# Turning K with 64x64 matmuls against the unit matrix in place of eight 128x128 transposes

## The chip, the cores and the metric

The kernel runs on one core of one Trainium2 chip. The metric is the device time of one execution in microseconds (us); lower is better. Five engines work side by side: TensorE (PE in the profile; PEld is its weight load), VectorE (DVE), ScalarE (ACT), GpSimd (POOL) and SyncE (SP, which issues most of the DMAs). Each works through its own list of instructions in order, and semaphores hold an instruction back until what it needs is there.

## The reference

An RWKV-6 attention is followed by a feed-forward block. All data are fp32.

```python
B, H, S, D = 4, 8, 768, 48
for t in range(S):                                   # per (b, h); state is D x D
    y[t]  = r[t] @ (state + outer(u * k[t], v[t]))
    state = w[t][:, None] * state + outer(k[t], v[t])
x = y.transpose(0, 2, 1, 3).reshape(B * S, H * D)    # 3072 x 384
h = x @ w_in                                         # 384 -> 2048
g = h * erf(softplus(h))
out = g @ w_out                                      # 2048 -> 384
```

## The kernel before

The sequence is cut into chunks of 128 tokens and the batch into pairs, which makes 12 steps, `s` = 0 to 11. A step handles one chunk of `NJ` = 2 batch elements with 8 heads each. Two heads share the 128 partitions: the heads of half `e` = 0 stand on partitions 0 to 47 and those of half `e` = 1 on 64 to 111. So `r`, `k` and `w` lie as [128, `JP` = 8, 128 tokens] with the head dimension on the partitions, `v` as [128 tokens, 16, 48], and `rows(e)` names the 48 partitions of a half.

**The attention of a step.** Inside a chunk, tokens are split into two halves `h` of 64 (`HC`). Products between tokens are formed by levels, from neighbouring tokens (level 1) to the halves of a 64 (level 6, `LOG`). For each level TensorE forms 32 small products, each in a 64x64 part of its array (`level_products`, L436); VectorE scales the operands for the next level (`scale`, L252) and VectorE or ScalarE takes the wanted part into `own` (`take_level`, L448 and L455). Then

- `from_own` (L470) multiplies `own` with `v` into the output `y`, 16 matmuls for each of its two calls (`swap` = 1 and 0);
- K is turned, so that tokens stand on the partitions: L663 into PSUM, and one ScalarE copy (L667) into `kT`;
- `state_part` (L522) multiplies `kT` with `v`, 32 matmuls, and VectorE and POOL make the state at the middle and at the end of the chunk from it (L690 to L695);
- `through_state` (L496) adds what the state gives to `y`, and the sum is copied into `xT` (L503 to L506, with small DMAs at L510).

Steps 0 to 4 (`DIRECT` = 4) do this in `attend`, and they alone turn K on TensorE. Steps 5 to 11 run `attend_late`, in which VectorE and POOL form the near terms from rows and `kT` comes by DMA (L405). At the head of `attend_late` for steps 6 to 11 stand, directly behind each other, `from_own` of the step before (L470), `level_products` (L436), the second `from_own` (L470) and `through_state` (L496) of the step before.

**The feed-forward block** runs in between, in pieces that `place` hands out: `hidden` (L731) forms the 16 tiles of `h` with three matmuls each for 256 tokens; ScalarE copies them out (L740) and applies softplus and erf (L713, L716); VectorE multiplies (L720); `project` (L754) multiplies with `w_out`, eight matmuls at a time. `hidden` works for step s - 1 and `project` for step s - 3. In steps 0 to 3 the two weight matrices are converted from 64-bit words as well (`convert`: ScalarE L207 and L209, VectorE L216 and L219, POOL L223). In step 0 a few extra matmuls on constant data stand at L623 and L631.

**What sets the order.** The whole program runs under `tc.manual_schedule`: each engine's instructions stand in the order in which the Python code emits them, with no planner. Around the changed lines, TensorE's order in step 2 is `from_own` (swap 1), the turn, twelve matmul rows of L731, `state_part`, `from_own` (swap 0), twelve rows of L731, `through_state`. In steps 3 and 4 there are 24 and 36 rows of L731 behind the turn; in step 0 there is one matmul of L631 instead. PSUM results of the attention go to two buffers of two banks each, taken in turn by `products`.

An fp32 matmul shows in the trace as two weight loads and two matmul rows; a transpose as one of each.

Of the kernel before, what the change touches and what calls it, by code (L numbers as in the profile page):

```python
# [17 lines left out]
P = 128  # L18
EP = 64
HC = 64  # L20
NC = 2
# [39 lines left out]
def kernel(  # L61
# [14 lines left out]
    nc = tc.nc  # L76
    PSUM = bass.MemoryType.PSUM

    n_steps, _, _, JP, C = rkw.shape
    NH, D = v.shape[2:]  # L80
    NP = JP // NJ
    NE = NH // JP
# [32 lines left out]
    ident = const.tile([P, P], FP32, name="ident")  # L115
# [12 lines left out]
    def products(shape):  # L128


        n = 0 if turns["converting"] else turns["next"]
        turns["next"] = 1 - n
        return ps_p.tile(shape, FP32, name=f"pp{n}")
# [31 lines left out]
    def near_log(s):  # L165
        return NEAR_LOG - (s == DIRECT)
# [70 lines left out]
    def rows(e, n=D):  # L237
        return slice(e * EP, e * EP + n)
# [7 lines left out]
    def scale(s, level):  # L246

        in_t, tots = loaded[s][0], ready[s][1]
        half, nb = 1 << (level - 1), JP * C >> level
        n = 1 if s > DIRECT and level == LOG else 2  # L250
        halves = view(in_t[:, 0:2], half, [[JP * C - half, n], [2 * half, nb], [1, half]])
        nc.vector.tensor_mul(  # L252
            halves, halves, view(tots[level - 1], 0, [[1, n], [2, nb], [0, half]])
        )
# [165 lines left out]
    def parts_of(s):  # L420

        c, i = divmod(s, SPC)
        in_t, vt = loaded[s]
        made, tots, tot = ready[s]
        ends = tot.rearrange("p (n h) -> p n h", h=NC)
        return c, in_t, vt, made, states[i][c % 2], states[i][1 - c % 2], ends

    def level_products(pp, rk, level):

        half = 1 << (level - 1)  # L430
        m = HC if level <= MASKED else half
        for n in range(JP):
            for s0 in range(0, C, HC):
                for e in range(NE):
                    t0 = s0 if level <= MASKED else s0 + half
                    nc.tensor.matmul(  # L436
                        pp[s0 : s0 + m, e, n, :m],
                        lhsT=rk[rows(e), 1, n, s0 : s0 + m],
                        rhs=rk[rows(e), 0, n, t0 : t0 + m],
                        start=True,  # L440
                        stop=True,
                    )

    def take_level(own, pp, level):
        half = 1 << (level - 1)
        got = pp[:].rearrange("p e n t -> p (e n) t")
        if level <= MASKED:
            nc.vector.copy_predicated(  # L448
                rights(own[:], half),
                rights(mask_sb[:, level - 1 : level, :].to_broadcast([P, NH, HC]), half),  # L450
                rights(got, half),
            )
        else:
            for s0 in range(0, C, HC):
                nc.scalar.copy(own[s0 : s0 + half, :, half:], got[s0 : s0 + half, :, :half])  # L455
# [74 lines left out]
    def spread_blocks(s, pp):  # L530


        n = D // 2
        for e in range(NE):
            nc.tensor.matmul(
                pp[:EP, e, 0:2, HC // 2 : HC // 2 + n],
                lhsT=over_blocks[rows(e)].rearrange("p b n -> p (b n)"),
                rhs=ident[rows(e), rows(e)], start=True, stop=True,
            )
        few = att.tile([EP, NE * 2, n], FP32, name="few", bufs=1)  # L540
        nc.scalar.copy(
            few[:].rearrange("p (e i) d -> p e i d", e=NE),
            pp[:EP, :, 0:2, HC // 2 : HC // 2 + n],
        )
        g_rows = dram.tile([C // NEAR, JP * NE * D], FP32, name="g_rows")
        nc.sync.dma_start(
            out=g_rows[:].rearrange("b (n d) -> (b n) d", n=JP),
            in_=few[:].rearrange("p i d -> p (i d)"),
        )
        spread[s] = att.tile([P, JP, NE, D], FP32, name="spread", bufs=1)  # L550
        nc.sync.dma_start(
            out=spread[s][:].rearrange("p n e d -> p (n e d)"),
            in_=g_rows[:, None, :].to_broadcast([C // NEAR, NEAR, JP * NE * D]),
        )
# [55 lines left out]
    def attend(s, xT, place, behind):  # L610

        c, in_t, vt, made, S, S_next, ends = parts_of(s)
        K = in_t[:, 1]
        RK = in_t[:, 0:2]


        following = prepare(s + 1) if s + 1 < n_steps else iter(())
        own = made if s >= DIRECT else att.tile([P, NH, HC], FP32, name="own")

        def keep_busy(*columns):  # L620
            zeros = states[1][0][:].rearrange("p n d -> p (n d)")
            for n in columns if not s else ():
                nc.tensor.matmul(  # L623
                    y[:].rearrange("p e j q t -> p (e j q t)")[:, :n], lhsT=ident[:],
                    rhs=zeros[:, :n], start=True, stop=True, skip_group_check=True,
                )

        def stay_warm(times=1, where=None):
            for _ in range(times):
                ps = where or ps_m.tile([P, NP * C], FP32, name="m")  # L630
                nc.tensor.matmul(  # L631
                    ps[:], lhsT=ident[:], rhs=ws[s][:, :NP], start=True, stop=True
                )

        if s == DIRECT:
            next(following)
        for level in range(near_log(s) + 1 if s == DIRECT else 1, LOG + 1):
            rk = made[:] if level == 1 else RK
            pp = products([P, NE, JP, HC])
            level_products(pp, rk, level)  # L640
            if level == LOG and s == DIRECT:
                spread_blocks(s + 1, pp)
            scale(s, level)
            keep_busy(DM, DM // 2)
            if level == 1 and s == 1:
                stay_warm()
            got = pp[:].rearrange("p e n t -> p (e n) t")
            if level == 1:
                if not s:
                    nc.vector.tensor_copy(out=first[:], in_=mask_sb[:, 0, :])  # L650
                nc.vector.tensor_mul(
                    own[:], got, first[:, None, :].to_broadcast([P, NH, HC])
                )
            else:
                take_level(own, pp, level)
            if level > 1 and (s, level) != (DIRECT, LOG - 1):
                next(following, None)
            place(level - 1)

        from_own(s, own, 1)  # L660
        ps = products([P, JP, P])
        for n in range(JP):
            nc.tensor.transpose(ps[:, n, :], K[:, n, :], ident[:])  # L663
        if not s:
            stay_warm()
        kT = att.tile([P, NH, D], FP32, name="kT", bufs=1)
        nc.scalar.copy(  # L667
            kT[:].rearrange("p (e n) d -> p e n d", e=NE),
            ps[:].rearrange("p n (e d) -> p e n d", e=NE)[..., :D],
        )  # L670
        if c:
            nc.gpsimd.tensor_mul(
                faded[0][:], S[:], ends[:, :, 0:1].to_broadcast([P, JP, D])
            )
        next(following, None)
        place(LOG)


        if s:
            ps = products([P, NC, JP, HC])  # L680
            ps = [ps[:, h] for h in range(NC)]
        else:
            ps = [ps_m.tile([P, JP, HC], FP32, name="m") for h in range(NC)]
        state_part(s, kT, ps)
        from_own(s, own, 0)
        if not s:
            stay_warm(1, products([P, NP * C]))
        for e in range(NE):
            if c:
                nc.vector.tensor_add(middle[rows(e)], faded[0][rows(e)], ps[0][rows(e), :, :D])  # L690
            else:
                nc.vector.tensor_copy(middle[rows(e)], ps[0][rows(e), :, :D])
        nc.gpsimd.tensor_mul(faded[1][:], middle[:], ends[:, :, 1:2].to_broadcast([P, JP, D]))
        for e in range(NE):
            nc.vector.tensor_add(S_next[rows(e)], faded[1][rows(e)], ps[1][rows(e), :, :D])  # L695
        for _ in following:
            pass
        place(LOG + 1)
        through_state(s, xT)
        behind()  # L700
# [127 lines left out]
    with tc.manual_schedule(  # L828
# [20 lines left out]
        for s in range(n_steps):  # L849
# [31 lines left out]
            if s > DIRECT:  # L881
                attend_late(s, place)
                continue
            attend(s, xTs[s], place, lambda: convert_at(LOG + 2))
            if s + 2 < n_steps:
                load_step(s + 2)
# [108 lines left out]
```

## Time and profile before

| | |
|---|---|
| median of 11 runs | 621.29 us (620.39 to 623.63) |
| profiled execution | 620.52 us, of which the span of the trace is 618.7 us |
| PE busy | 602.8 us, 97% of the span, 6,858 matmul rows and as many weight loads |
| VectorE, ScalarE, POOL busy | 411.1, 293.5 and 292.0 us (66%, 47%, 47%) |
| the chain that ended last | PE 83%, VectorE 7%, DMA 3% |
| the turn of K | 40 transposes, 273 ns each, and five ScalarE copies of 800 ns |
| DMA | 63.27 MB, mean 102 GB/s |

The profile is one execution on the chip. A line such as `L731 PE MATMUL` names the source line, the engine and the operation, then output and inputs, the partitions and elements of each, and how often it ran. Matmuls are pipelined: one starts long before the one ahead of it has ended, so the duration of one (273 ns for a transpose) is more than the time it holds the engine. The time that a group holds TensorE is read from its start to the start of the group behind it. "issue" ahead of a row means that the engine waited for nothing that the profile shows.

### The profile page before, as it was taken

The page shows a single profiled execution, that of the slowest core. Times are in us where ns is not written, and L with a number is a line of the kernel's source. Part 1 is how long each engine was busy: PE and PEld are TensorE (multiplying, and loading weights), DVE is VectorE, ACT ScalarE, POOL GpSimd, SP SyncE. Part 2 cuts the span into 40 slices and gives each one's busy share as a digit, 9 for nine tenths or more (in the row PEclk, how much of TensorE's full clock was granted, in tenths as well). Part 3 has the DMA queues.
Part 4 walks back from the last instruction along what each step waited for, and adds up shares of the span by engine and source line. Part 5 has one row for each costly group of instructions (what it writes and reads, how often), then busy time and mean ns, then how long its engine had stood idle before and what let it go on. Part 6 is the DMA issues. An engine that isn't in the chain of part 4 may idle for free.

```text
span 618.7 us, 15587 instructions
## 1 busy us (share of the span) xinstructions
PE 602.8 (97%) x6858; PEld 445.8 (72%) x6858; DVE 411.1 (66%) x459; ACT 293.5 (47%) x374; POOL 292.0 (47%) x295
## 2 busy tenths in 40 slices
PE   7989999999999999999999999999999999999997
PEld 6667787578668768668768768768768768668654
DVE  5697697894995897897697797797797311110300
ACT  2547878625536634443543543543543543634600
POOL 4348184601497389299189299299297000000000
PEclk9999999999999999999999999999999999999999
DMA  8376481440333405515416415415402100000000
GB/s 326 121 275 199 163 258 44 193 146 11 136 104 107 123 28 173 125 36 172 101 63 178 114 43 177 121 37 143 120 36 68 35 26 1 8 25 1 0 26 25
DMA packets 51371, 63.27 MB, mean 102 GB/s; under 512 B 34920, under 2 KB 40296, under 8 KB 49896
## 3 DMA queue, kind: packets, MB, share of 16 engines
q1 hardware_dynamic: 50152, 61.68, 31.6%
q8 instruction: 54, 0.88, 0.6%
q10 hardware_dynamic: 1152, 0.59, 0.4%
q14 instruction: 13, 0.11, 0.1%
HBM read 52.39 MB, written 8.69 MB: 99 GB/s over the span
## 4 chain that ended last, share of the span: by engine, by line
PE 83%; DVE 7%; DMA 3%; POOL 2%; issue 2%; ACT 2%; SPq 1%; DVEq 0%; POOLq 0%; ACTq 0%
PE m L731 37%; PE m L754 36%; PE pp L436 5%; DVE in L252 2%; DMA in<-in_rkw 2%; PE y L470 2%; PE pp L522 1%; PE y L496 1%; DMA w<-in_rkw 1%; POOL tot_sb L304 1%; PE pp L663 1%; DVE sums L356 1%; DVE pp L216 1%; DVE words L370 1%; DVE own L448 1%
## 5 line engine op out<-in xcount | busy, mean ns | idle before, releaser
L731 PE MATMUL m<-xT,w_in_sb 128*128 128x256 f32 x1152 | 257.2, 382 | 1.4 <-DVE w_in_sb L219 1.2
L754 PE MATMUL m<-w_out_sb,h 128*128 128x384 f32 x768 | 252.4, 488 | 1.3 <-POOL w_out_sb L223 1.3
L731 PEld LDWEIGHTS m<-xT,w_in_sb 128*128 128x128 f32 x1152 | 216.1, 190 | 33.7 <-issue 2.4
L754 PEld LDWEIGHTS m<-w_out_sb,h 128*128 128x128 f32 x768 | 144.5, 190 | 100.1 <-POOL w_out_sb L223 1.9
L740 ACT COPY h<-m 128x512 f32<-128x512 f32 x96 | 55.9, 583 | 128.3 <-PE m L731 128.2
L720 DVE TENSOR_TENSOR h<-h,sp 128x1024 f32<-128x1024 f32 x48 | 75.1, 1605 | 51.6 <-ACT sp L716 51.4
L252 DVE TENSOR_TENSOR in<-in,tot_sb 128x1024 f32<-128x1024 f32 (+1 forms) x60 | 85.8, 1438 | 30.0 <-PE pp L436 28.1
L370 POOL TENSOR_TENSOR words<-words,rest 128x528 f32<-128x528 f32 (+10 forms) x77 | 85.7, 1112 | 6.0
L366 POOL TENSOR_TENSOR rk<-words 128x528 f32<-128x528 f32 (+3 forms) x28 | 44.5, 1589 | 82.3 <-DVE sums L356 71.8
L763 ACT COPY o<-m 128x384 f32<-128x384 f32 x24 | 11.5, 480 | 113.1 <-PE m L754 113.1
L304 POOL TENSOR_TENSOR tot_sb<-tot_sb 128x256 f32<-128x256 f32 (+4 forms) x60 | 53.6, 893 | 4.5
L713 ACT ACTIVATE sp<-h 128x2048 f32<-128x2048 f32 x24 | 45.9, 1912 | 0.3
L716 ACT ACTIVATE sp<-sp 128x2048 f32<-128x2048 f32 x24 | 45.9, 1911 | 0.3
L436 PEld LDWEIGHTS pp<-in 48*64 48x64 f32 (+1 forms) x2368 | 33.8, 126 | 16.6 <-issue 9.9
L436 PE MATMUL pp<-in 48*64 48x64 f32 (+1 forms) x2368 | 38.4, 212 | 4.0 <-DVE own L448 1.4
L356 DVE TENSOR_REDUCE sums<-words 128x6 f32<-128x288 f32 (+8 forms) x66 | 29.2, 469 | 19.4 <-POOL words L366 19.1
L716 ACT ACT_TABLE_LOAD x24 | 30.8, 1283 | 15.3 <-issue 15.1
L366 POOL TENSOR_TENSOR words<-words 128x336 f32<-128x336 f32 (+6 forms) x49 | 35.1, 716 | 3.8
L356 DVE TENSOR_REDUCE sums<-rk 128x14 f32<-128x672 f32 (+9 forms) x54 | 34.8, 703 | 0.2
L713 ACT ACT_TABLE_LOAD x24 | 30.8, 1283 | 4.6 <-issue 4.2
L370 DVE TENSOR_TENSOR words<-words,rest 128x576 f32<-128x576 f32 (+8 forms) x34 | 27.9, 819 | 1.2
L223 POOL TENSOR_TENSOR w_out_sb<-w_out_sb,rest 128x768 int32<-128x768 int32 x8 | 17.8, 2232 | 18.3 <-DVE w_out_sb L219 18.3
(80 smaller groups left out, 437.5 us busy)
## 6 DMA issues: line engine op xcount, KB each, us to landing
in<-in_rkw SPq DMA_DIRECT2D x11, 1024.0 KB, 5.4
words<-in_moe_w_in SPq DMA_DIRECT2D x8, 768.0 KB, 4.6
words<-in_moe_w_out SPq DMA_DIRECT2D x8, 768.0 KB, 5.8
words<-in_rk_rows SPq DMA_DIRECT2D x8, 768.0 KB, 6.7
w<-in_rkw SPq DMA_DIRECT2D x11, 512.0 KB, 8.3
v<-in_v SPq DMA_DIRECT2D x12, 384.0 KB, 5.9
out<-o SPq DMA_DIRECT2D x24, 192.0 KB, 1.9
rest<-in_w_rows SPq DMA_DIRECT2D x8, 384.0 KB, 8.4
```

The lines of the kernel that those rows point to most:

```text
L252: nc.vector.tensor_mul(halves, halves, view(tots[level - 1], 0, [[1, n], [2, nb], [0, half]]))
L304: nc.gpsimd.tensor_mul(new, pair[:, :, 0], pair[:, :, 1])
L356: nc.vector.tensor_reduce(out=view(sums[:], n, [[near * (NEAR + 1), NEAR // near], [NEAR + 1, near - n]]), in_=terms[n], axis=mybir.AxisLi ...
L366: engine.tensor_mul(terms[n], r[:, :, n:], k[:, :, : near - n])
L370: engine.tensor_mul(k[:, :, :m], k[:, :, :m], w[:, :, n : n + m])
L436: nc.tensor.matmul(pp[s0 : s0 + m, e, n, :m], lhsT=rk[rows(e), 1, n, s0 : s0 + m], rhs=rk[rows(e), 0, n, t0 : t0 + m], start=True, stop=True,)
L713: nc.scalar.activation(held[0][:], h[:], AF.Softplus)
L716: nc.scalar.activation(held[0][:], held[0][:], AF.Erf)
L720: nc.vector.tensor_mul(h[:, part], h[:, part], held[0][:, part])
L731: nc.tensor.matmul(ps[:, ff, :], lhsT=w_in_sb[:, g * FG + f + ff, kk * P : (kk + 1) * P], rhs=xT[:, kk, :], start=kk == 0, stop=kk == KT - 1,)
L740: nc.scalar.copy(h[:, f : f + FT, :], ps[:])
L754: nc.tensor.matmul(ps[j][:], lhsT=gs[g][:, f, j * C : (j + 1) * C], rhs=w_out_sb[:, g * FG + f, :], start=g + f == 0, stop=g == NG - 1 and ...
```

## The change

In the five steps that turn K on TensorE, each of the eight 128x128 transposes (both halves, all tokens, with the unused partitions 48 to 63 and 112 to 127) is replaced by four plain matmuls. Each takes K of one half `e` and of 64 tokens, 48 x 64, as the stationary operand and the 48 x 48 unit matrix of that half as the moving one, and so leaves the 64 x 48 piece of K turned in PSUM. The layout in PSUM changes from [n, (e d)] to [e, n, d], with each half `e` in a bank of its own, and the ScalarE copy reads it in the new order. The moved lines behind it stand seven lines lower in the changed file: L731 becomes L738, L754 becomes L761, and the turn itself stands at L667 with its copy at L674.

```diff
         from_own(s, own, 1)
-        ps = products([P, JP, P])
+
+        ps = products([P, NE, JP, HC])
         for n in range(JP):
-            nc.tensor.transpose(ps[:, n, :], K[:, n, :], ident[:])
+            for h in range(NC):
+                for e in range(NE):
+                    t = slice(h * HC, (h + 1) * HC)
+                    nc.tensor.matmul(
+                        ps[t, e, n, :D], lhsT=K[rows(e), n, t], rhs=ident[rows(e), rows(e)],
+                        start=True, stop=True,
+                    )
         if not s:
             stay_warm()
         kT = att.tile([P, NH, D], FP32, name="kT", bufs=1)
         nc.scalar.copy(
             kT[:].rearrange("p (e n) d -> p e n d", e=NE),
-            ps[:].rearrange("p n (e d) -> p e n d", e=NE)[..., :D],
+            ps[:, :, :, :D],
         )
```

## The prediction

> **What bounds the kernel now.** I read the page first: engines, DMA queues, chain of waits.
>
> ```profile
> PE 602.8 (97%) x6858; PEld 445.8 (72%) x6858; DVE 411.1 (66%) x459; ACT 293.5 (47%) x374; POOL 292.0 (47%) x295
> ...
> q8 instruction: 54, 0.88, 0.6%
> ...
> PE 83%; DVE 7%; DMA 3%; POOL 2%; issue 2%; ACT 2%; SPq 1%; DVEq 0%; POOLq 0%; ACTq 0%
> PE m L731 37%; PE m L754 36%; PE pp L436 5%; DVE in L252 2%; DMA in<-in_rkw 2%; PE y L470 2%; PE pp L522 1%; PE y L496 1%; DMA w<-in_rkw 1%; POOL tot_sb L304 1%; PE pp L663 1%; DVE sums L356 1%; DVE pp L216 1%; DVE words L370 1%; DVE own L448 1%
> ```
>
> TensorE (PE) is busy 97% of the span and holds 83% of the chain that ended last, nearly all in the two feed-forward products, L731 and L754. So what PE itself gains or loses between 35 and 615 us counts one for one, unless PE is waiting just then. Remember q8 as well: 54 packets and 0.88 MB are 16 KB each, and PE has 13,808 rows in the trace (6,858 matmuls, as many loads, 92 semaphore rows), so one packet for each 256 of them. This queue brings PE its own instructions.
>
> Then the changed line, L663, and PE's timeline around one of its five uses (step 2):
>
> ```profile
> L663 PEld LDWEIGHTS pp<-ident,in x40: 138/141/143, 26.0 to 188.0; 128*128 128x128 f32 x40
> L663 PE MATMUL pp<-ident,in x40: 272/273/329, 26.1 to 188.1; 128*128 128x128 f32 x40
> ```
>
> ```profile
> 93.28 0.65 PE L470 MATMUL y<-own,v 64*48 64x64 f32 x28 [0.28 <-ACT own L455]
> 93.86 1.09 PE L663 MATMUL pp<-ident,in 128*128 128x128 f32 x8
> 94.79 2.76 PE L731 MATMUL m<-xT,w_in_sb 128*128 128x256 f32 x12
> 97.48 0.94 PE L522 MATMUL pp<-v,kT 64*48 64x48 f32 x64
> 98.23 0.63 PE L470 MATMUL y<-own,v 64*48 64x64 f32 x32
> 98.79 2.86 PE L731 MATMUL m<-xT,w_in_sb 128*128 128x256 f32 x12
> 101.58 0.66 PE L496 MATMUL y<-in,s 48*48 48x64 f32 x32
> ```
>
> Columns: start, time until the last of the group ended, and how many. Ends overlap, so I count from start to start. Eight transposes hold PE from 93.86 to 94.79, **0.93 us**, the same in all five steps. The chain in order of time has them in steps 1 to 4 (59.53, 93.93, 143.05, 187.38, each 1.02 us) and not in step 0. The neighbours are the price list: 64 rows are 32 small fp32 matmuls, each two loads and two matmul rows, where a transpose is one of each (x8). L522 (48 columns loaded, 48 streamed) takes 0.75 us here, L496 (48, 64) about 0.93.
>
> Last, PE's timeline in step 6 and in step 10, where the waits view says "issue", a wait for nothing that the profile shows:
>
> ```profile
> 250.77 0.67 PE L470 MATMUL y<-own,v 64*48 64x64 f32 x32
> 251.25 1.11 PE L436 MATMUL pp<-in 48*64 48x64 f32 x64
> 252.19 0.63 PE L470 MATMUL y<-own,v 64*48 64x64 f32 x32
> 252.63 0.63 PE L496 MATMUL y<-in,s 48*48 48x64 f32 x32
> 253.08 0.45 PE L496 MATMUL y<-in,middle 48*48 48x64 f32 x17
> 254.51 0.44 PE L496 MATMUL y<-in,middle 48*48 48x64 f32 x15 [0.98 <-issue]
> ```
>
> ```profile
> 439.04 0.51 PE L496 MATMUL y<-in,s 48*48 48x64 f32 x21
> 439.77 0.37 PE L496 MATMUL y<-in,s 48*48 48x64 f32 x10 [0.23 <-issue]
> ```
>
> In the middle of one run of L496, whose operands were all ready, PE stops, at 253.5 for 0.98 us and at 439.5 for 0.23. Counted from start to start, this L496 block takes 2.24 and 1.54 us in place of 1.00 as in steps 7, 8 and 11: losses of 1.24 and 0.53, together 1.77 us. I numbered PE's rows in order of time (loads, matmuls and semaphore rows). The stops come before rows 7616 and 11456, and two more in step 0 (14.75 and 20.78 us) before rows 448 and 704. All four are 192 modulo 256. PE resumes 2.36 and 2.54 us after a q8 packet started (252.15 and 437.23). So these are waits for instructions, at every 256th row, where small matmuls use rows up faster than packets come.
>
> [...]L470 to the transposes takes 0.56 to 0.59 us from start to start (142.39 to 142.98), L470 to tiled L436 0.48 (250.77 to 251.25); the twelve L731 after transposes take 2.69, after tiled L470 2.79.
> [...]
>
> **The change part by part.** The program order of both kernels is equal on all five engines, and every wait too, apart from these matmuls. No DMA is moved, no queue passed.
>
> (1) Removed: 8 transposes in each of five steps, 0.93 us.
>
> (2) Added: 32 matmuls loading 64 columns and streaming 48, a form that the trace lacks. Floor: L522 (48, 48), 0.86 us where a wide matmul follows (276.55 to 277.41). Ceiling: L436 (64, 64) with the same neighbours, 1.04 (31.00 to 32.04). L496 (48, 64) takes 1.00, so sixteen more loaded columns cost 0.04 and sixteen more streamed ones 0.14. I take 0.86 + 0.04 = 0.90.
>
> (3) [...]L470 gets shorter by 0.11, L731 behind it longer by 0.10.
>
> Per step 0.90 - 0.93 - 0.11 + 0.10 = -0.04 us, from -0.08 to +0.10. Four steps on the chain: **-0.16** (-0.3 to +0.4).
>
> Costed at nothing: the ScalarE copy L667 reads the same 768 elements in another order (800 ns); behind it twelve or more L731 cover it (step 1: copied by 61.4, used at 63.08). If the copy slipped more than 1.6 us, L522 would be late next. Step 0 gains nothing: its copy starts at 27.29 because ScalarE is converting weights until 27.27. No other engine's instructions change, so VectorE, POOL and SP have nothing to cost.
>
> (4) **More instructions.** A step's turn had 16 rows and gets 32 x 4 = 128: +112. After step 4 everything stands 560 rows later, 48 modulo 256. Block borders fall 48 rows earlier in the code, or 208 later, in all of steps 5 to 11. This is the edit's largest term.
>
> Where it counts: the run L470, L436, L470, L496 at the head of steps 6 to 11, 384 rows in 2.87 us with nothing slow between. In the slow stretches ahead, 256 rows last some 20 us. A packet starts about 1.0 us after PE reached the 300th row ahead of its border (251.15 to 252.15; 299.06 to 300.13; 345.70 to 346.83) and its rows can run 2.4 us later: 3.4 us in all. Only a border over some 290 rows deep in this run, and not past its end, comes too early. Depth of the border, from my numbering:
> - before: steps 6 to 11 at 355, 405, 199, 249, 299, 413. Stops at 355 and 299 only, as seen.
> - after, 48 less (or 208 more, past the end): 307, 357, 407, 201, 251, 365. Stops in steps 6, 7, 11.
>
> Slope between the two measured: (1.24 - 0.53)/56 rows = 0.0127 us a row. So 307 gives 0.63, 357 gives 1.27, 365 gives 1.37: 3.27 us, 1.77 before: **+1.5 us**. PE is the chain there, nothing hides it. The two measured packets vary by 0.2 us; I bound the term at +0.5 and +2.2. The shorter run L436, L535, L522 (248 rows, 1.4 us) had no stop with borders in it and gets none.
>
> Steps 0 to 4: step 0's two stops precede the change. New borders there: one in L522 of step 0, due at 28.82 while its packet (start 26.58, 0.96 us long) can be used at about 28.9: +0.05, passed on through POOL's L693, which has 0.04 of slack. The next, in L436 of step 1 at 31.8, would wait 0.6 or more, covered by L731, which waits for VectorE until 34.4; that cover ends at some 1.4 us. With DMA loaded (57% in this stretch) packets start up to 3.4 us after their row instead of 1.0, as at 41.48; then up to 1 us would show. Both sides: 0 to +1.0, I take +0.05.
>
> Sum: -0.16 + 1.5 + 0.05 = **+1.4 us**. The profiled execution is 620.52 us, 618.7 of span and 1.8 around it, so 621.9; the median of the runs is 621.29, 0.77 above it, so 622.7.
>
> **Rivals.** About 0.2%, 1.24 us, is what a measurement of this kernel can tell from no change.
>
> A. As above: waits for instructions move into three deep places. 622.7, chance 0.50.
>
> B. The same mechanism, mildly: the stop at 307 doesn't happen, or packets come sooner, so stops stay near 1.8 to 2.4 us, with the direct saving. -0.2 to +0.6, 621.1 to 621.9. For it: depth 299 lost only 0.53, the edge is near. Against: two borders lie as deep as the costly one. Chance 0.26.
>
> C. Turn at its ceiling (+0.4), and packets in steps 0 and 1 delayed by weight loads (+1.0) on top of A's 1.5: 624.2. For it: late packets at 41.48 and 75.71; against: waits for VectorE cover most. Chance 0.14.
>
> D. Faster: packets start about 1 us earlier than I take, so that the deep stops nearly vanish. For it: the packet at 437.23 started 0.37 us after its row (436.86), not 1.0; the lag is not fixed. With 1.0 us less the three stops lose 0, 0.27 and 0.37 us, 0.64 against 1.77 before: -1.1 - 0.16 = -1.3, 620.0; with none at all -1.9, 619.4. It decides from about 0.9 us, where the gain passes 0.2%. Against: three other packets in this run lagged 1.07, 1.13 and 0.94. Chance 0.10.
>
> That the turn isn't what it says: it must give the same kT, and the order of all else is unchanged, so no rival there.
>
> **The numbers.** A's own spread, 0.5 to 2.2 us, is partly under 1.24: of its 0.50 some 0.10 fall within 0.2%. Slower 0.40 + 0.14 + a little of B = 0.56; same 0.10 + 0.24 = 0.34; faster 0.10. Likeliest 622.7, own range 621.8 to 623.5. Range 620.9 to 624.2 leaves out D and the tails.
>
> **What would show it.** Right: turn blocks of 0.86 to 1.04 us with 64 rows; L470 ahead of them 0.48; L731 behind them longer by 0.10; an "issue" stop inside L496 in steps 6, 7 and 11, none in step 10; PE's rows 14,368 and 56 packets in q8. Wrong: no stop in steps 7 and 11; a turn over 1.1 us; a wait of L522 for the copy; new PE idle time in steps 0 to 2.

## The result, and the profile after

The changed kernel takes **629.27 us** (median of 12 runs, 623.7 to 635.4) against 620.95 for the kernel before (median of 47). The ratio is **1.0108, 95% interval 1.0091 to 1.0125**; two runs at 634 and 635 us, whose clock was granted at 0.987, are left out of it, which makes 6.7 us. So it is slower, as forecast, but by 8 us at the median where 1.4 was said, and outside the range.

The profiled execution is one of the quicker ones: 624.91 us, span 623.1, against 620.52 and 618.7. It holds 4.4 us of the loss; a second profile, below, holds 10.3. First the page of the kernel after:

```profile
PE 605.0 (97%) x7138; PEld 448.1 (72%) x7138; DVE 410.4 (66%) x459; ACT 293.6 (47%) x374; POOL 292.7 (47%) x295
...
q8 instruction: 56, 0.92, 0.6%
...
PE 85%; DVE 6%; issue 3%; DMA 2%; POOL 2%; ACT 2%; SPq 0%; DVEq 0%; POOLq 0%; ACTq 0%
PE m L738 38%; PE m L761 35%; PE pp L436 5%; DVE in L252 2%; PE y L470 2%; PE y L496 2%; PE pp L522 1%; POOL tot_sb L304 1%; DMA w<-in_rkw 1%; DMA in<-in_rkw 1%; PE pp L667 1%; DVE sums L356 1%; DVE words L370 1%; DVE own L448 0%; DVE rk L366 0%
```

PE is busy 2.2 us longer, its share of the chain is larger, and q8 brought 56 packets: 14,368 rows in place of 13,808, as counted. The changed line, and PE's timeline around it in step 3:

```profile
L667 PEld LDWEIGHTS pp<-ident,in x320: 129/135/135, 25.7 to 189.2; 48*64 48x64 f32 x160
L667 PE MATMUL pp<-ident,in x320: 205/218/247, 25.7 to 189.3; 48*64 48x48 f32 x160
```

```profile
143.50 0.67 PE L470 MATMUL y<-own,v 64*48 64x64 f32 x32
143.98 1.10 PE L667 MATMUL pp<-ident,in 48*64 48x48 f32 x64
145.01 5.45 PE L738 MATMUL m<-xT,w_in_sb 128*128 128x256 f32 x24
150.39 0.80 PE L522 MATMUL pp<-v,kT 64*48 64x48 f32 x52
```

The turn holds PE for 1.03 us (143.98 to 145.01), not 0.93. L470 ahead of it takes 0.48, not 0.59, and the 24 rows of L738 behind it 5.38, where the kernel before had 5.28. A step's turn thus costs 1.03 - 0.93 - 0.11 + 0.10 = 0.09 us more.

Late in the run, PE's timeline in step 6, then in step 7:

```profile
253.48 0.63 PE L470 MATMUL y<-own,v 64*48 64x64 f32 x32
253.93 0.56 PE L496 MATMUL y<-in,s 48*48 48x64 f32 x25
255.89 0.27 PE L496 MATMUL y<-in,s 48*48 48x64 f32 x4 [1.41 <-issue]
```

```profile
302.32 0.50 PE L496 MATMUL y<-in,middle 48*48 48x64 f32 x18
304.17 0.43 PE L496 MATMUL y<-in,middle 48*48 48x64 f32 x14 [1.34 <-issue]
```

PE stops in the middle of L496 at rows 8128, 9152 and 12992, in steps 6, 7 and 11, the three that were named; all are 192 modulo 256, and step 10 has no stop. From start to start the three L496 blocks take 2.67, 2.66 and 2.46 us in place of 1.00: 4.8 us, where 1.8 were lost before.

Early in the run there is something new in step 1:

```profile
31.29 1.03 PE L436 MATMUL pp<-rk 48*64 48x64 f32 x57
34.39 0.34 PE L436 MATMUL pp<-rk 48*64 48x64 f32 x7 [2.06 <-issue]
34.66 1.52 PE L631 MATMUL m<-w,ident 128*128 128x512 f32 x2
35.98 4.09 PE L738 MATMUL m<-xT,w_in_sb 128*128 128x256 f32 x12
```

PE stands still for 2.06 us before row 1472, seven rows short of the end of L436, level 1. What follows shows in the windows view (busy time of PE, PEld, DVE, ACT and POOL, then the granted share of PE's clock, DMA share, GB/s):

```profile
30.00:35.00 5.00, 2.94 (x99) 1.93 (x99) 3.97 (x6) 1.53 (x5) 1.34 (x3) 1.00 0.39 151
35.00:39.00 4.00, 4.00 (x10) 2.73 (x9) 3.60 (x4) 1.74 (x3) 2.54 (x2) 0.57 0.88 301
```

From 35 to 39 us the clock was granted at 0.57: the trace's clock record has half speed for 3.4 us from 35.25. In the kernel before, this window stood at 1.00.

The account of this execution, by the times at which PE starts the same code: the first L761 of step 5 starts at 208.65, before 207.36 (+1.3 us: the four turns' 0.36, and the stop in step 1 with the half clock behind it); from there to the last row of L761 it takes 410.57 us, before 407.48 (+3.1 us: late stops). Together +4.4. The other four of the 8 us at the median are not in this profile.

### The profile page after: what moved, and what is told of

Same layout as the page of the kernel before. It is cut to its first block, busy times and chain, and to the rows that moved or that the text cites. A ratio compares the mean times of both kernels' runs of the same rounds, so it can differ in the third digit from the quotient of the medians.

```text
span 623.1 us, 16147 instructions
## 1 busy us (share of the span) xinstructions
PE 605.0 (97%) x7138; PEld 448.1 (72%) x7138; DVE 410.4 (66%) x459; ACT 293.6 (47%) x374; POOL 292.7 (47%) x295
## 4 chain that ended last, share of the span: by engine, by line
PE 85%; DVE 6%; issue 3%; DMA 2%; POOL 2%; ACT 2%; SPq 0%; DVEq 0%; POOLq 0%; ACTq 0%
PE m L738 38%; PE m L761 35%; PE pp L436 5%; DVE in L252 2%; PE y L470 2%; PE y L496 2%; PE pp L522 1%; POOL tot_sb L304 1%; DMA w<-in_rkw 1%; DMA in<-in_rkw 1%; PE pp L667 1%; DVE sums L356 1%; DVE words L370 1%; DVE own L448 0%; DVE rk L366 0%
## 5 line engine op out<-in xcount | busy, mean ns | idle before, releaser
L738 PE MATMUL m<-xT,w_in_sb 128*128 128x256 f32 x1152 | 258.3, 383 | 0.1
L761 PE MATMUL m<-w_out_sb,h 128*128 128x384 f32 x768 | 252.4, 488 | 1.3 <-POOL w_out_sb L223 1.3
L738 PEld LDWEIGHTS m<-xT,w_in_sb 128*128 128x128 f32 x1152 | 217.4, 191 | 32.3 <-issue 1.1
L761 PEld LDWEIGHTS m<-w_out_sb,h 128*128 128x128 f32 x768 | 144.5, 190 | 100.1 <-POOL w_out_sb L223 1.9
L252 DVE TENSOR_TENSOR in<-in,tot_sb 128x1024 f32<-128x1024 f32 (+1 forms) x60 | 84.4, 1415 | 32.1 <-PE pp L436 30.2
L304 POOL TENSOR_TENSOR tot_sb<-tot_sb 128x256 f32<-128x256 f32 (+4 forms) x60 | 51.9, 865 | 4.5
L436 PEld LDWEIGHTS pp<-in 48*64 48x64 f32 (+1 forms) x2368 | 33.8, 125 | 15.3 <-issue 9.4
L436 PE MATMUL pp<-in 48*64 48x64 f32 (+1 forms) x2368 | 38.4, 212 | 2.7 <-DVE in L252 1.3
```

The lines of the kernel that those rows point to most:

```text
L252: nc.vector.tensor_mul(halves, halves, view(tots[level - 1], 0, [[1, n], [2, nb], [0, half]]))
L304: nc.gpsimd.tensor_mul(new, pair[:, :, 0], pair[:, :, 1])
L436: nc.tensor.matmul(pp[s0 : s0 + m, e, n, :m], lhsT=rk[rows(e), 1, n, s0 : s0 + m], rhs=rk[rows(e), 0, n, t0 : t0 + m], start=True, stop=True,)
L738: nc.tensor.matmul(ps[:, ff, :], lhsT=w_in_sb[:, g * FG + f + ff, kk * P : (kk + 1) * P], rhs=xT[:, kk, :], start=kk == 0, stop=kk == KT - 1,)
L761: nc.tensor.matmul(ps[j][:], lhsT=gs[g][:, f, j * C : (j + 1) * C], rhs=w_out_sb[:, g * FG + f, :], start=g + f == 0, stop=g == NG - 1 and ...
```

## The experiments

**Two theories.** Theory 1: the 560 additional rows move the places at which PE needs a new block of 256 instructions; where these fall among small matmuls PE waits, and the clock may drop behind a long wait. Theory 2: the 64x64 matmuls are dearer than transposes by themselves, in time or in what they do to PE's clock. Shifting rows tells them apart without touching the turn, and a number of rows can be taken out or put in at three places: in the warm-up at the start, in step 1, and in steps 2 to 4.

**1. The changed kernel, 48 rows fewer at the start.**

```diff
-        for _ in range(20):
-            nc.tensor.matmul(warm[:], lhsT=ident[:], rhs=ident[:], start=True, stop=True)
+        for n in (3, 3, 3, 3, 2, 2, 2, 2):
+            nc.tensor.matmul(
+                warm[:, :n], lhsT=ident[:], rhs=ident[:, None, :].to_broadcast([P, n, P]),
+                start=True, stop=True,
+            )
```

> The changed kernel with 48 PE rows fewer ahead of everything: the 20 warm-up matmuls of 128 columns become 8 of 384 or 256 (same 2560 columns), so that every later row stands 48 places earlier and the 256-row borders of steps 5 to 11 fall where the kernel before has them. Theory 1 (waits for instructions at the borders, and the lower clock they bring, are the loss): stops in steps 6 and 10 only, 1.2 and 0.5 us, none in step 1, no clock loss behind 5 us; the turn itself costs 4 x 0.09; about 0.4 us over before, within 0.2%, spread like before. Theory 2 (the 64x64 matmuls themselves, by their duration or by what they do to TensorE's clock, are the loss): the median stays near the changed kernel's, 1.0% over before.

Measured: 625.79 us, ratio 1.0068 (1.0050 to 1.0087). The profile, 620.14 us, is just what theory 1 said: stops late in steps 6 and 10 only, none in step 1, clock 1.0, and 407.73 us from step 5's first L761 to the last. But 16 of the 20 runs took 624 to 630 us, with mean clocks of 0.991 to 0.997. So theory 1 has the late part right, and something else, early and not in every run, costs 5 us.

**2. The kernel before, 48 rows more at the start** (32 warm-up matmuls of 80 columns in place of 20 of 128).

> The kernel before, transposes and all, with 48 PE rows more ahead of everything: 32 warm-up matmuls of 80 columns in place of 20 of 128 (same 2560 columns). The borders of steps 5 to 11 fall where the changed kernel has them, those of step 1 do not. Theory 1: stops in steps 6, 7 and 11 of 1.66, 1.65 and 1.45 us, 4.8 against 1.8 before: +3.0 us (0.5%) with no 64x64 turn at all; if long stops late in the run also lower the clock, the runs' clocks fall under 1.0 and the median is up to 4 us higher still. Theory 2: as before, within 0.2%.

Measured: 631.87 us, 1.0166 (1.0140 to 1.0193). Not a clean trial: with the narrower warm-up the clock stayed at half until 20.6 us, and the first L436 starts at 15.55 us instead of 8.16, so the time says little and the late part has to be read alone. Behind that, the kernel with its transposes has the changed kernel's late stops. Its timeline in steps 6 and 7:

```profile
258.19 0.56 PE L496 MATMUL y<-in,s 48*48 48x64 f32 x25
259.99 0.27 PE L496 MATMUL y<-in,s 48*48 48x64 f32 x4 [1.25 <-issue]
```

```profile
306.42 0.50 PE L496 MATMUL y<-in,middle 48*48 48x64 f32 x18
308.51 0.43 PE L496 MATMUL y<-in,middle 48*48 48x64 f32 x14 [1.59 <-issue]
```

The third stop is in step 11 (1.25 us). Step 5's first L754 to the last takes 410.74 us, 3.3 more than before. The late loss needs no 64x64 turn.

**3. The changed kernel, 208 rows more in steps 2 to 4.**

```diff
+        for i in range({2: 18, 3: 18, 4: 16}.get(s, 0)):
+            n, h, e = i // 4, i // 2 % 2, i % 2
+            t = slice(h * HC, (h + 1) * HC)
+            nc.tensor.matmul(
+                ps[t, e, n, :D], lhsT=K[rows(e), n, t], rhs=ident[rows(e), rows(e)],
+                start=True, stop=True,
+            )
```

> The changed kernel with 52 of the turn's matmuls given twice (18 in step 2, 18 in step 3, 16 in step 4), 208 rows more: the borders of steps 5 to 11 fall where before has them, the border in step 1 stays where the changed kernel has it. Theory 1: the stop in step 1 stays (2 us, with half clock behind it for 3.4 us), late stops in steps 6 and 10 only. The repeated matmuls cost 52 x 33 ns = 1.7 us, so direct: 0.4 + 1.3 + 1.7 = 3.4 us over before; if the lower clock of single runs comes from the stop in step 1, clocks spread as in the changed kernel (0.987 to 0.997), if it comes from the late stops, they stay at 0.997. Theory 2: more small matmuls, so slower than the changed kernel, +1.2% or more over before.

Measured: 628.48 us, 1.0107 (1.0077 to 1.0137). The late part is back at 407.37 us, yet the whole is as slow as the changed kernel, 7.7 us over before: 4.3 over the sum of 3.4, and 4.7 if the turns are counted once, since the 1.3 in it has them already. The missing loss is early, again. The stop in step 1 is there, 2.34 us, but with no half clock behind it; half clock stands at 16.68 us for 3.4 us and at 74.71 for 6.8.

**4. The kernel before, one piece of L754 inside the run of small matmuls.**

```diff
         if before:
+            piece(projs, s - 3)
             from_own(before, ready[before][0], 0)
...
+        if DIRECT + 1 < s < n_steps:
+            order = ("APPAPP", *order[1:])
```

> The kernel before with one piece of the second feed-forward product (four matmuls of L754, 1.3 us) moved from just behind the run of small matmuls at the head of steps 6 to 11 into it, between the first and the second half. Same rows, same borders. Theory 1: 300 rows ahead of a border then last over 3.4 us, so the stops in steps 6 and 10 go: -1.7 us (0.3% faster than before), if the later xT and loads stay covered. Theory 2 has nothing to say of it; if the stops were something else than waits for instructions, they stay, and the time is as before.

Measured: 620.98 us, 1.0006 (0.9991 to 1.0021). In its profile no stop is left in steps 6 to 11, with every border at the row number it had; this is the strongest evidence that the stops come from too many small matmuls in a row. But it gains nothing. Its timeline in step 6:

```profile
252.85 1.11 PE L436 MATMUL pp<-in 48*64 48x64 f32 x64
253.89 2.85 PE L755 MATMUL m<-w_out_sb,h 128*128 128x384 f32 x8
256.67 0.66 PE L470 MATMUL y<-own,v 64*48 64x64 f32 x32
```

L436 to the wide L755 takes 1.04 us, where L436 to L470 took 0.94, and behind the wide piece the small matmuls begin once more. What this costs can be read in step 11, which has no stop in either kernel: from its first L470 to the first matmul of the next `hidden` (L732 here, L731 before) it takes 25.59 us (485.50 to 511.09) against 25.24 (483.98 to 509.22). That is 0.35 us a step, 2.1 us in six steps, for 1.8 saved, and step 5's first L755 to the last takes 407.75 us, as before.

**5. A second profile of the changed kernel.**

> The changed kernel once more, for a second profile: its runs span 623.7 to 635 us. Theory 1 expects the stops at the same rows (in step 0 before rows 448 and 704, in step 1 before row 1472, late in steps 6, 7, 11), with other lengths, and half clock right behind the longer ones; theory 2 expects the difference to lie in the turns.

Measured: 630.78 us, 5.9 over the first profile. The stops are at the same rows (1.73 us before row 1472 by the starts around it, 2.28 in the first profile). The 5.9 us arise in step 2. PE's timeline there, then SP's queue:

```profile
68.44 1.16 PE L436 MATMUL pp<-rk 48*64 48x64 f32 x64 [0.89 <-DVE s L702]
69.53 1.56 PE L738 MATMUL m<-xT,w_in_sb 128*128 128x256 f32 x6
71.89 1.41 PE L738 MATMUL m<-xT,w_in_sb 128*128 128x256 f32 x4 [0.80 <-DMA xT<-y]
75.96 3.75 PE L738 MATMUL m<-xT,w_in_sb 128*128 128x256 f32 x8 [2.66 <-DMA xT<-y]
79.64 1.80 PE L436 MATMUL pp<-in 48*64 48x64 f32 x64
```

```profile
68.56 2.44 SPq L510 DMA_DIRECT2D xT<-y  x3
71.12 0.51 SPq L194 DMA_DIRECT2D words<-in_moe_w_out  x1
```

L738 waits for xT, 0.80 and 2.66 us, and gets it by 76 us; the first profile had no gap there. The three small DMAs of xT (L510) took SP 2.44 us to issue, 1.78 in the first profile; ScalarE's three took 3.34, 2.13 in the first. Behind them SP issues transfers of 768 and 1024 KB. ScalarE's line stands beside SP's:

```profile
68.57 3.34 ACTq L510 DMA_DIRECT2D xT<-y  x3
```

ScalarE began the last of its three at 71.04 us and ended it at 71.91, while SP issued L194 from 71.12 on; it landed at 75.82, 3.9 us later, and L738 went on at 75.96. In the first profile its last one had ended at 70.83 and landed 1.25 us later. The windows view then shows the clock (columns as above):

```profile
74.00:78.00 4.00, 2.04 (x5) 1.72 (x6) 0.85 (x1) 3.23 (x5) 1.83 (x1) 0.53 1.00 417
78.00:82.00 4.00, 4.00 (x72) 3.05 (x71) 0.48 (x1) 2.33 (x2) 0.00 (x0) 0.61 0.90 364
```

0.53 and 0.61: half speed for 6.8 us from 74.27 in the clock record. Behind the stop in step 1, 1.52 us of idle time, there is none this time. What goes with the slower issue? A q8 packet started at 69.36, in the middle of it; in the first profile it started at 67.96 and had ended at 68.89, 0.2 us after the first DMA was begun at 68.69.

**6. Experiment 1's kernel, a second profile.**

> The changed kernel with 48 rows fewer ahead, once more, for a second profile: 3 of its 20 runs took under 621 us at full clock and the others 624 to 630 at 0.991 to 0.999, and the profile shown is one of the three. A profile of the common kind should show where: theory 1 expects a stretch of half clock between 14 and 45 us behind a wait of over 1 us for instructions in step 0 or 1; theory 2 expects the half clock behind the turns of steps 1 to 4.

Measured: 626.03 us. (Of the 20 runs two, not three, had taken under 621 us, and two more 621.6.) No half clock in steps 0 and 1, where theory 1 expected it, and none behind the turns of steps 3 and 4: it is at 74.07, for 6.8 us, behind waits of L738 in step 2 of 0.57 and 3.30 us. The packet started at 68.78, and L510 took SP 2.20 us. Over all profiles, with a packet starting within the issue of L510 SP needs 2.20 to 2.94 us for it (starts 68.44, 68.78, 69.36, 69.42, 70.25, 70.59: 2.94, 2.20, 2.44, 2.65, 2.74, 2.77), and with none 1.78 or 1.79 (the eight others).

But a slow issue alone is not the loss. The slowest of all is in experiment 1's first profile, the one of 620.14 us at full clock:

```profile
67.37 2.94 SPq L510 DMA_DIRECT2D xT<-y  x3
```

The six profiles fall into two kinds. In three (this one, the second of the changed kernel, experiment 3) the packet started 0.80 to 0.86 us after the first L510; ScalarE was done issuing its last L510 0.3 us after SP had issued the first big load, it landed 3.9 to 4.6 us later, PE waited 3.5 to 4.1 us in all, and 6.8 us of half clock followed. In the other three (experiment 1's first, experiments 7 and 12) it started 1.07 to 1.40 us after the first L510; ScalarE was done 0.1 us before SP began the big load, its last L510 landed in 1.5 us, and PE waited 1.1 to 1.3 us and kept its full clock there. By these six profiles, what costs is that the last piece of xT falls behind the big load.

**7. Transposes in step 0 alone.**

```diff
+        if not s:
+            ps = products([P, JP, P])
+            for n in range(JP):
+                nc.tensor.transpose(ps[:, n, :], K[:, n, :], ident[:])
...
+            for i in range(48 if s == 4 else 32):
+                n, h, e = i // 4 % JP, i // 2 % 2, i % 2
```

> 64x64 matmuls turn K in steps 1 to 4 alone; step 0 keeps its transposes. 16 of step 4's turning matmuls are given twice, so that 512 rows are added in all and the borders of steps 5 to 11 fall where before has them; everything up to step 1's turn stands where before has it. Theory 1 (borders): no stop in step 1, late stops in steps 6 and 10 as before; it costs 4 x 0.09 for the turns and 16 x 0.033 for the repeated ones, so +0.9 us (0.15%) over before, clocks spread as before. Theory 2 (the matmul form itself costs time or clock): still most of the changed kernel's loss, +5 us or more. If it is step 0 that suffers from the form, +0.9 too, which then speaks for both; the two looks at the other kernels tell these apart.

Measured: 622.99 us, 1.0048 (1.0023 to 1.0072): 2.6 us, not 0.9, with most clocks at 1.0. The late part is as before (407.33). The step-1 stop is gone, but a packet started at 70.59, within the issue of L510, and L744, which is L738 here, waited 1.14 us. A miss of the number: the packet fits the cause found in 5 and 6, but how much of the other 1.7 us it makes was not measured.

**8. A pair for the hand-over: the same 208 rows as in experiment 3, but 8 of the 52 matmuls in step 1** (8, 15, 15, 14 in place of 0, 18, 18, 16).

> As the kernel with 52 repeated turning matmuls (18, 18 and 16 in steps 2 to 4), but with 8 of them in step 1 (8, 15, 15, 14): the same rows, the same late borders, the same stop in step 1. Only the border at the hand-over from step 1 to step 2 moves 32 rows earlier, so that its packet of instructions starts at about 65 us, as before, and not at 68 to 70 us, while the six small DMAs of xT (L510) are issued. Theory 1, extended: the long wait of L738 for xT in step 2 (2.7 us and more) and the half clock of 6.8 us behind it go; 623 to 625 us in place of 628.5. If the packet at the hand-over is not the cause: 628 again.

Measured: **624.30 us**, 1.0050 (1.0028 to 1.0072), against 628.48 in experiment 3; all seven runs are under 625.4, five of the six there over 627. The packet started at 68.02, not at 65 as expected, but 2.4 us ahead of the issue, which came later too. SP's queue and PE's timeline at the same place:

```profile
70.47 1.79 SPq L510 DMA_DIRECT2D xT<-y  x3
```

```profile
71.43 4.54 PE L745 MATMUL m<-xT,w_in_sb 128*128 128x256 f32 x18
```

1.79 us again, and 18 rows of L745 without a gap. The stop in step 1 is there as in the first profile of the changed kernel, 2.06 us, this time with 6.8 us of half clock behind it. Where a packet falls at this hand-over is worth 4 us. The borders of steps 2 to 4 move as well, by 32, 20 and 8 rows; behind the hand-over, up to step 5, they show at most one idle time of 0.2 us for instructions (experiment 3, step 4).

**9. All borders at harmless places: 48 rows fewer at the start, 80 more in step 1, 176 more in steps 2 to 4.**

> The changed kernel with 48 rows fewer at the start (no stop in step 1), 20 repeated turning matmuls in step 1 (the hand-over's packet where before has it) and 44 in steps 2 to 4 (late borders where before has them). Theory 1, extended: nothing but the turns' 4 x 0.09 us and the 64 repeated matmuls at 33 ns, 2.1 us, is left: 2.5 us over before (0.4%), clocks near 1.0 as before. If the 64x64 matmuls cost more than their own time: 5 us or more over before.

Measured: 623.10 us, 1.0038 (1.0027 to 1.0049), all but 2 of 17 runs at a mean clock of 0.999 or more. 2.2 us over its reference, where 0.36 for the turns and 2.1 for the repeated matmuls were summed. This fells theory 2: with the 64x64 turn in all five steps and more of its matmuls, nothing is left of the 8 us but their own time.

The medians also give an estimate of the two early losses. From what each kernel takes over before I subtract 0.36 us for the turns, 33 ns for each repeated matmul and, in the changed kernel, 3.1 us for the late stops. There remain 4.9 us in the changed kernel and 5.7 in experiment 3, which have both the stop in step 1 and the packet at the hand-over; 4.7 in experiment 1, which has the packet alone; 1.3 in experiment 8, which has the stop alone; and -0.3 here, with neither.

**10. The kernel before, 32 rows fewer at the start** (8 warm-up matmuls of 256 and 4 of 128 columns).

> The kernel before, transposes and all, with 32 rows fewer at the start (12 warm-up matmuls with the same 2560 columns): the packet at the hand-over from step 1 to step 2 now falls among the DMAs of xT, as in the changed kernel, and late only one border lies deep (331, in step 10), so late stops are worth 1.2 us in place of 1.8. Theory 1, extended: many runs wait for xT in step 2 and then run at half clock, clocks 0.994 to 0.997 in place of 0.997 to 1.0, median 2 to 5 us over before with no 64x64 turn at all. Theory 2: as before or 0.6 us faster.

Measured: 621.74 us, 1.0023 (1.0005 to 1.0040). Slower, with single runs at 627 and 629 and 6 of 22 mean clocks at 0.996 or less, where none of the 38 of before is under 0.997, but far from 2 to 5 us at the median: a partial miss. In its profile the packet started at 68.30, 0.8 us ahead of L510, and did no harm, and its half clock, 3.4 us, stands in step 0; how often the packet does harm was not measured. One more miss is in it, in step 6:

```profile
255.06 0.59 PE L754 MATMUL m<-w_out_sb,h 128*128 128x384 f32 x1
256.46 0.91 PE L754 MATMUL m<-w_out_sb,h 128*128 128x384 f32 x2 [0.81 <-issue]
```

The border lies 387 rows deep, 3 past the end of the run, two rows of L754 behind it, and PE still loses 1.1 us between two L754 that otherwise start 0.33 apart. So a border 3 rows past the end of the run still cost time here.

**11. The kernel before, a second profile.**

> The kernel before once more, for a second profile. Theory 1 expects stops before rows 448, 704, 7616 and 11456 again, of other lengths within some 0.3 us, its packet at the hand-over at 65 to 66 us, and the DMAs of xT issued in 1.8 us.

Measured: 620.68 us. Stops before rows 448, 704 and 7616 again, and a short one before 11456, depth 299: the L496 block there takes 1.24 us, so 0.24 are lost where the first profile lost 0.53. That depth is the edge: in the eight profiles with a border there the loss is 0.2 to 0.6 us, where depth 307 lost 1.5 to 1.8. L510 took 1.79 us.

**12. The unit matrix widened to 64 columns.**

```diff
-                        ps[t, e, n, :D], lhsT=K[rows(e), n, t], rhs=ident[rows(e), rows(e)],
+                        ps[t, e, n, :], lhsT=K[rows(e), n, t], rhs=ident[rows(e), rows(e, EP)],
```

> The changed kernel with the moving unit matrix widened from 48 to 64 columns (the added columns give zeros that nobody reads), rows unchanged: 64 loaded, 64 streamed. If the loaded columns set the pace, as the 14.0 ns a row of the changed kernel against 14.2 for L436 suggests, the turn stays at 1.03 to 1.06 us; if loaded and streamed columns add up, as the prediction's 0.90 assumed, it grows by 0.14 a turn. Stops at the same rows as in the changed kernel.

Measured, in step 3:

```profile
144.35 0.67 PE L470 MATMUL y<-own,v 64*48 64x64 f32 x32
144.83 1.11 PE L667 MATMUL pp<-ident,in 48*64 48x64 f32 x64
145.88 5.45 PE L738 MATMUL m<-xT,w_in_sb 128*128 128x256 f32 x24
```

1.05 us with 64 streamed columns, 1.03 with 48. With 64 columns loaded, sixteen more streamed ones cost 0.02 us a turn, where the prediction had taken 0.14 from L522 and L496.

## Why the prediction was wrong, point by point

**Right: the largest named term and its places.** Program order alone gave the shift of 560 rows, the packets, and all three steps of the late stops. Every sign that it named for being right came. The sign of the change followed, but only 3.1 of the 8 us for the reason given, and "new PE idle time in steps 0 to 2", which it named for being wrong, came too. Experiments 1, 2, 3 and 9 each moved the late stops as the row numbers say: the late part takes 407 to 408 us in one set of kernels and 410.6 to 410.8 in the other, whichever way K is turned.

**Term (4), late, under-sized by half.** Said +1.5, measured +3.1. The slope between two measured depths (299 and 355) failed: at depth 307 the stop cost 1.67, not 0.63. Depth 299 was the edge itself, with 0.53 in one profile and 0.24 in another, so the line through it was too low. Eight rows further in the whole stop is paid, and it does not grow with depth: 1.5 to 1.8 us at 307, 1.2 to 1.5 at 355, 1.5 to 1.7 at 365, over all profiles.

**Term (4), steps 0 to 4, failed in its cover.** Said +0.05 in all, with up to 1.0 if DMA was loaded. The stop in step 1 was foreseen in its place, a wait of 0.6 us or more in L436, but put at nothing because 1.4 us of it would be covered; it took 2.06 us, more than the cover, and half clock behind it (3.4 us) was not thought of at all. The early part cost +1.3 us in the first profile, turns included. That the half clock comes from the stop is argued from its place and not shown: of the five profiles with this stop, three have half clock right behind it (3.4 us after waits of 2.06 and 1.52 us, 6.8 after 2.06) and two have none (1.52 and 2.34 us).

**The step that failed outright: "No DMA is moved, no queue passed."** The prediction went on that SP had "nothing to cost". The instruction packets stand among the DMA queues (q8, 54 packets before and 56 after), and they are moved: the one at the hand-over starts at 65.30 us in the first profile before and at 67.96 in the first after. One came to lie among the six DMAs of xT at the hand-over from step 1 to step 2, and with it SP needed 2.20 to 2.94 us to issue its three, 1.78 or 1.79 without; in three profiles the last of the six then landed 3.9 to 4.6 us after its issue, behind the start of a big load, and PE waited 3.5 to 4.1 us, with 6.8 us of half clock behind. That the packet slows the issue is argued from these times and was not shown by itself. This is 4 us between two kernels with the same matmuls, 8 of which stand in another step (experiments 3 and 8), and 5.9 us between two profiles of the changed kernel, so it can account for a median 4 us above the first profile and for runs up to 631 us. The two runs at 634 and 635 us have no profile and stay unexplained. No rival had it; rival C, the nearest, had late packets, but as PE's own wait.

**Terms (1) to (3), small but of the wrong sign.** Removed 0.93, and -0.11 for L470 and +0.10 for L738 beside the turn, were exact. The added turn was 1.03, at the ceiling of 1.04, not 0.90: 0.90 added the cost of more loaded columns to that of more streamed ones, an estimate that experiment 12 does not bear out (0.02 us for sixteen more streamed columns, where 0.14 was taken). +0.36 us for four steps in place of -0.16; the sum in experiment 9 agrees.

**The range** was made from bounds on terms that all stood in PE's queue. With the hand-over and the half clock missing, no bound reached 629.

**Open:** why the issue of six small DMAs takes 0.4 to 1.2 us longer with a packet starting within it, and in what share of runs; and what decides whether half clock follows a wait. A version faster than both was not found: taking the late stops away (experiment 4) cost about as much at the added changes between small and wide matmuls (2.1 us) as it saved (1.8).

## What to carry to other kernels

When an edit changes how many instructions TensorE has, number its rows and look where the blocks of 256 begin after it (here 56 packets of 16 KB for 14,368 rows): here every later border moved, by 560 rows after step 4, and a border 307 to 365 rows deep in a run of 384 rows of small matmuls cost 1.2 to 1.9 us each time. Look also at what the packet itself runs into, here six small DMAs that PE waited for, up to 4.1 us where the last of them fell behind a big load, and at what PE's clock does behind a wait: here half speed for 3.4 or 6.8 us behind some of them. Before a small edit is judged by its time, shift the kernel by a few rows and measure again: here the shift cost some twenty times what the turn itself does (8 us against 0.36).

## What the runs showed of the hardware

- In the first profiles of the kernels before and after, a wait for instructions ends 2.3 to 2.7 us after the start of its packet (11 stops, four before and seven after).
- With warm-up matmuls of 80 columns PE's clock was at half until 20.6 us (experiment 2); with 128, 256 and 384 columns and the same sum it was full by 4.5 to 7.3 us in the other profiles (128 columns: 4.65 before, 4.53 after).
- Half clock came in stretches of 3.4 or 6.8 us (3.4 from 35.25 us in the first profile after, 6.8 from 74.27 in the second), experiment 2 with its slow warm-up and the end of the run apart. In step 0 it came for 3.4 us, from 16.2 to 16.7 us on, in the four profiles in which PE idled 1.0 to 1.3 us before row 448 (experiments 3, 4, 7 and 10, two of them kernels with transposes), and in none of the others, experiment 2 apart, where it idled 0.93 us or less (0.72 before, 0.93 after).
- The length of a wait alone does not say whether half clock follows: in step 2, waits of 1.1 to 1.3 us left the clock full (three profiles) and 6.8 us of half clock stood behind waits of 3.5 to 4.1 us in two pieces (three profiles), but behind the stop in step 1 a wait of 1.52 us was followed by half clock in one profile and not in another.
